# Two batches by halves: a sliding-window attention with a feed-forward layer, its first loads, casts and transposes cut in two

## The chip, the cores and the metric

The kernel runs on one core of a Trainium2 chip. The metric is the device time of one execution in microseconds (us). The core has a matrix engine (TensorE, PE in the profile, with PEld for its weight loads), VectorE (DVE), ScalarE (ACT), GpSimd (POOL) and SyncE (SP), which here only issues DMAs. Each engine works through its own queue in order; semaphores tie the queues together.

## The reference

```python
# q, k, v: [8 batches, 8 heads, 576 tokens, 64], float32
scores = q @ k.T / 8                                   # per batch and head
scores = where(|i - j| <= 32, scores, -1e9)            # a band of 65 keys a query
attn   = softmax(scores) @ v
x      = attn transposed and reshaped to [4608, 512]   # 8 heads side by side
h      = x @ w_in                                      # [4608, 2048]
out    = maximum(0.01 * h, h) @ w_out                  # [4608, 512], float32
```

## The kernel before, in words

Heads go in pairs: two heads of 64 fill 128 partitions, so a batch has four pairs (`NPAIR`). The work is a chain of **steps**, one pair and one stretch of tokens each. Steps 0 to 15 (`OLD`) belong to batches 0 and 1: a batch has two halves of 288 tokens (`HALF`), and steps 0 to 3 are half 0 of batch 0, pair by pair, 4 to 7 its half 1, 8 to 15 batch 1. Steps from 16 on take four blocks of 64 tokens of batches 2 to 7 in another form (`score_blocks`, `product_blocks`), with queries and keys transposed by DMA. The parts of an early step:

- `score`: TensorE multiplies blocks of 64 keys with the queries that can see them into the one score tile `ps`, ScalarE takes the exponential into `e`, GpSimd multiplies with a mask (line 442) into one of six `prob` tiles.
- `sums`: TensorE sums over keys with a block matrix of ones (line 466), VectorE takes the reciprocal (line 471).
- `product`: TensorE multiplies with values (line 482) into the one tile `x`; `scaled`: VectorE multiplies with the reciprocal (line 496) into `xT`, the input of the feed-forward layer.

For batches 0 and 1, `load_qk` (line 80) brings a pair's queries and keys as float32 with 96 partitions of six tokens, `cast_qk` (lines 279 and 281) makes bfloat16 of them in `qb` and `kb`, and `transposes` turns them on TensorE (line 327), with ScalarE taking them out of the accumulators (lines 335 and 341). Queries and keys of a pair are separate tiles, and the queries of batches 0 and 1 are kept apart by even and odd tokens. Values come by `load_v` (line 104) in two DMAs of 64 partitions a pair, and `cast_v` puts them into a block-diagonal tile `vbd` that was cleared before. Batch 1 has block-diagonal keys `kbd` too (`place_keys`, line 359). SP issues all these loads in program order; the weights go by GpSimd's queue (`load_w_in`, line 675, and `load_w_out`, line 679), each in four pieces, cast on the way.

The feed-forward layer takes **groups** of tokens: groups 0 to 3 are the four halves of batches 0 and 1. For each of 16 tiles `f` of 128 hidden features, TensorE adds four chunks (one per pair, line 520), and ScalarE applies the leaky ReLU (`h_out`, line 531) into `gT`. `h_first` opens four tiles at once and goes chunk by chunk, so that a chunk can begin when its pair is done. Output tiles of 128 tokens take 16 matmuls with `w_out` (lines 593 and 609).

The order is written out by hand up to the end of group 1: casts, transposes, `score`, `sums`, `product` and `scaled` of batch 0, with dummy matmuls (`keep_busy`, line 622) in between; then the tiles of group 0 with steps 4 to 7 (`second_half`) among them; then group 1 with transposes of batch 1 (`second_pair`) and the score of step 8. From there a plan interleaves the tiles with the steps: `spend` is called before each tile or quarter of an output tile (a **turn**), runs the steps that are due (step 8 in the seventh turn, 9 in the ninth, then 10 and 11), and in the first turns some extra work of batch 1. `step` also casts and transposes queries and keys of batch 2 and later by `qk_due` and issues later loads by `qk_next`, `v_next`. Batch 2's transposed queries are copied into `qz` by `place_queries` (line 315); `qz`, `kz` and `vw` of batches 2 and up share memory (two `sets`) with the tiles of batches 0 and 1, and the zeros in `qz` are written by `clear_half` (lines 234 and 239).

The opening of the order before, which sets when the loads are asked for:

```python
load_qk(0, 0); load_qk(0, 1); load_v(0, 0)
load_qk(0, 2); load_qk(0, 3)
for p in range(1, NPAIR):
    load_v(0, p)
```

Of the kernel before, what the change touches and what calls it, by code (L numbers as in the profile page):

```python
# [16 lines left out]
def kernel(  # L17
# [14 lines left out]

    nc = tc.nc
# [12 lines left out]
    EVEN = HALF // 2  # L46
# [22 lines left out]
    def load_qk(b, p, behind=None):  # L69

        for into, src, name in ((qf, q, "qf"), (kf, k, "kf")):
            t = fload.tile([96, 2, RUN * D], FP32, name=f"{name}{p}")
            if behind is not None:
                behind.memset(t[0:1, 0, 0:1], 0.0)
                behind = None
            heads = src[b, 2 * p:2 * p + 2]
            if b < BY_DMA:
                nc.sync.dma_start(out=t, in_=heads.rearrange("a (p c) d -> p a (c d)", c=RUN))  # L80
            elif into is qf:
# [9 lines left out]
            into[b, p] = t  # L91
# [9 lines left out]
    def load_v(b, p):  # L101
        t = vf[b, p]
        for a in range(2):
            nc.sync.dma_start(
                out=t[64 * a:64 * a + 64],
                in_=v[b, 2 * p + a].rearrange("(c p) d -> p c d", p=64),
# [28 lines left out]
    qb = const.tile([96, NPAIR, RUN, 2, D], BF16)  # L135
    kb = const.tile([96, NPAIR, RUN, 2, D], BF16)
# [5 lines left out]
    qT, kbd, vbd, qz, kz, vw, vw_two = [], [], [], [], [], [], []  # L142
    for t, at in zip(sets, (0, NPAIR * S)):
        qT.append(sets[0][:, at:at + NPAIR * S].rearrange("p (n s) -> p n s", n=NPAIR))
# [22 lines left out]
    def clear(t, p):  # L167
# [4 lines left out]

    mask = [const.tile([128, 2, 2, EVEN], BF16, name=f"mask{i}") for i in range(2)]
    nc.vector.memset(mask[0][:, 1, :, 0:16], 0.0)
    nc.vector.memset(mask[1][:, 1, :, 128:EVEN], 0.0)
# [7 lines left out]
        [((0, 0, 48), (2, 48, 64), (4, 112, 32)), ((1, 16, 64), (3, 80, 64))],  # L183
        [((4, 0, 32), (6, 32, 64), (8, 96, 48)), ((5, 0, 64), (7, 64, 64))],
    ]

    win = sets[1][:, N_SET - 384:].rearrange("p (c m i) -> p c m i", c=2, m=3)
    nc.gpsimd.memset(win, 1.0)
    for lo in (0, 64):
# [3 lines left out]
            base=0, channel_multiplier=-1, pattern=[[1, 2], [0, 3], [2, 64]],  # L193
# [3 lines left out]
            base=2 * W, channel_multiplier=1, pattern=[[-1, 2], [0, 3], [-2, 64]],  # L197
        )
    nc.gpsimd.memset(vbd[0][:, 3], 0.0)
    win_f = win.rearrange("p c m i -> p c (m i)")  # L200

    def make_mask(hf):
        lo = (16, 32)[hf]
        nc.gpsimd.tensor_copy(out=mask[hf][:, 0], in_=win_f[:, :, lo:lo + EVEN])
        lo = (16, 0)[hf]
        nc.gpsimd.tensor_copy(out=mask[hf][:, 1, :, lo:lo + 128], in_=win_f[:, :, 0:128])
# [49 lines left out]
    prob = const.tile([128, NPROB, 2, 2, EVEN], BF16)  # L256
# [3 lines left out]
    ps_v = ps[:, P0:P0 + 2 * HALF].rearrange("p (n c i) -> p n c i", n=2, c=2)  # L260
# [14 lines left out]
    def cast_qk(b, p, q_eng=None):  # L275
        for eng, src, dst in ((q_eng or nc.gpsimd, qf, qb), (nc.gpsimd, kf, kb)):
            to, tok = dst[:, p], src[b, p].rearrange("p a (c d) -> p c a d", d=D)
            if eng is nc.scalar:
                eng.activation(out=to, in_=tok, func=AF.Copy)
            else:  # L280
                eng.tensor_copy(out=to, in_=tok)  # L281

    def cast_v(b, p, on_act=False, heads=range(2), eng=nc.gpsimd):
        for a in heads:
            r = slice(64 * a, 64 * a + 64)
            if on_act:
                nc.scalar.activation(out=vbd[b % 2][r, p, :, r], in_=vf[b, p][r], func=AF.Copy)  # L287
            else:
                eng.tensor_copy(out=vbd[b % 2][r, p, :, r], in_=vf[b, p][r])
# [8 lines left out]
    def transpose_dma(b, p):  # L298
        t = kt.tile([128, S], BF16, name="kT")
        for to, src in ((t, qb), (kz[b % 2][:, p, W:W + S], kb)):  # L300
            nc.sync.dma_start_transpose(
                out=to.rearrange("p (c i) -> p c i", c=RUN),
                in_=src[:, p].rearrange("p c a d -> p (c a d)"),
            )
        landing.append((base(b) - 4 + p, b, p, t))
# [12 lines left out]
    def transposes(b):  # L318

        for p in range(NPAIR):  # L320
            for which, src in (("q", qb), ("k", kb)):
                if (b, p) == (1, 2):
                    tp = xps.tile([128, RUN, 96], BF16, name="tp", tag="sx"[which == "q"])
                else:
                    tp = mmps.tile([128, RUN, 96], BF16, name="tp", tag="mm")
                for c in range(RUN):
                    nc.tensor.transpose(
                        tp[:, c],
                        src[:, p, c].rearrange("p a d -> p (a d)"),
                        ident[0:96, 0:96],  # L330
                    )

                tok = tp.rearrange("p (e c) i -> p c i e", c=2)
                if which == "q":
                    nc.scalar.activation(
# [568 lines left out]
```

## Time and profile before

| | before |
|---|---|
| median of three runs | 314.26 us (313.77 to 315.05) |
| the profiled execution | 314.13 us |
| its span in the profile | 312.3 us |
| TensorE busy | 298.2 us (95%) |
| VectorE busy | 221.6 us (71%) |
| ScalarE busy | 212.6 us (68%) |
| GpSimd busy | 199.1 us (64%) |
| DMA | 49.47 MB, mean 158 GB/s |
| matmuls of the hidden layer, line 520 | 133.2 us |
| output matmuls, line 593 | 122.5 us |

The span runs from the first to the last instruction that the profile holds; the time of an execution has 1.83 us more around it. Shares are of the span. A row of the timeline reads: start, length, engine, line and operation, output and input, and in brackets how long the engine had stood idle before it and what released it. A row of the windows reads: stretch, length, then busy time with number of instructions for PE, PEld, DVE, ACT and POOL, the granted clock of TensorE, the DMA share and GB/s. The queue q1 of the DMA view carries what SP issues, q0 what GpSimd issues.

### The profile page before, as it was taken

To read this page: it belongs to the slowest core of one execution; us is meant where nothing else is said; L and a number is where in the kernel's file an instruction comes from. 1 tells how busy PE (TensorE), PEld (TensorE's weight loads), DVE (VectorE), ACT (ScalarE), POOL (GpSimd) and SP (SyncE) were. 2 spreads that over 40 slices of the span, in tenths; PEclk is the share of its full clock that TensorE was granted. 3 is DMA by queue.
4 is the path that set the end of the run, shared out by engine and by line. 5 is a ranking of instruction groups with operands and counts; after the bars stand their busy time and mean duration, and the time that the engine had idled before them with its cause. 6 is when DMAs were issued, how large, how long until landed. Compare 5 with 4: busy or idle time off the path is not lost.

```text
span 312.3 us, 6748 instructions
## 1 busy us (share of the span) xinstructions
PE 298.2 (95%) x2516; PEld 194.8 (62%) x2545; DVE 221.6 (71%) x290; ACT 212.6 (68%) x434; POOL 199.1 (64%) x250
## 2 busy tenths in 40 slices
PE   1799999999999999999999999999999999999996
PEld 1577775585765858585959585858555555544643
DVE  3688959779768887898789767898679866743000
ACT  7687698583865858585949686858589548842731
POOL 7789936899799999488778357578947622110000
PEclk9999999999999999999999999999999999999999
DMA  8999999998999799989989995797950011001002
GB/s 181 224 217 227 268 249 198 204 216 143 211 216 216 145 266 174 206 174 251 198 145 186 257 230 101 163 209 144 206 129 0 33 67 41 0 36 68 34 28 75
DMA packets 122017, 49.47 MB, mean 158 GB/s; under 512 B 96256, under 2 KB 117504, under 8 KB 121984
## 3 DMA queue, kind: packets, MB, share of 16 engines
q1 hardware_dynamic: 117760, 44.84, 72.7%
q0 software_dynamic: 4224, 4.19, 8.0%
q8 instruction: 20, 0.33, 0.5%
q14 instruction: 13, 0.11, 0.1%
HBM read 36.70 MB, written 9.44 MB: 148 GB/s over the span
## 4 chain that ended last, share of the span: by engine, by line
PE 77%; POOL 10%; DMA 5%; ACT 3%; SPq 2%; issue 2%; DVE 1%; POOLq 0%; ACTq 0%; DVEq 0%
PE mm L520 34%; PE mm L593 31%; PE ps L380 3%; DMA kf<-in_k_dram 2%; PE mm L609 2%; POOL prob L387 2%; PE s L398 2%; POOL kb L281 2%; PE x L398 2%; POOL qb L281 2%; DMA set<-kb 1%; ACT set L287 1%; POOL prob L442 1%; DMA vbuf<-in_v_dram 1%; SPq L80 1%
## 5 line engine op out<-in xcount | busy, mean ns | idle before, releaser
L520 PE MATMUL mm<-xT,w_in_bf 128*128 128x256 bf16 (+3 forms) x956 | 133.2, 294 | 0.4
L593 PE MATMUL mm<-w_out_bf,gT 128*128 128x512 bf16 (+2 forms) x537 | 122.5, 373 | 1.3
L407 DVE RECIPROCAL r<-r 128x256 f32<-128x256 f32 (+1 forms) x56 | 94.9, 1696 | 37.3 <-ACT r L406 36.9
L520 PEld LDWEIGHTS <-w_in_bf 128*128 128x128 bf16 x960 | 91.4, 98 | 30.6 <-issue 0.6
L387 POOL TENSOR_TENSOR prob<-e,band 128x512 bf16<-128x512 bf16 (+1 forms) x56 | 62.6, 1117 | 56.0 <-ACT e L385 54.6
L593 PEld LDWEIGHTS <-gT 128*128 128x128 bf16 x560 | 52.0, 98 | 54.1
L531 ACT ACTIVATE gT<-mm 128x288 bf16<-128x288 f32 (+2 forms) x112 | 49.8, 479 | 12.3 <-PE mm L520 9.6
L385 ACT ACTIVATE e<-ps 128x512 bf16<-128x512 f32 (+1 forms) x56 | 32.4, 579 | 27.7 <-PE ps L380 27.0
L598 ACT ACTIVATE o_sb<-mm 128x512 f32<-128x512 f32 (+2 forms) x35 | 20.5, 585 | 38.5 <-PE mm L593 38.2
L554 ACT ACTIVATE gT<-mm 128x512 bf16<-128x512 f32 x64 | 35.7, 596 | 5.5 <-PE mm L520 4.2
L471 DVE RECIPROCAL r<-s 128x288 f32<-128x288 f32 x16 | 31.2, 1950 | 2.9 <-PE s L466 2.8
L281 POOL CAST kb<-kf 96x768 bf16<-96x768 f32 x32 | 27.2, 851 | 9.2 <-DMA kf<-in_k_dram 8.1
L411 DVE TENSOR_TENSOR xT<-x,r 64x256 bf16<-64x256 f32 (+1 forms) x56 | 24.3, 435 | 3.3
L411 DVE TENSOR_TENSOR xT<-s,r 64x256 bf16<-64x256 f32 (+1 forms) x56 | 24.3, 434 | 3.3
L442 POOL TENSOR_TENSOR prob<-e,mask 128x576 bf16<-128x576 bf16 x16 | 20.3, 1273 | 5.9 <-ACT e L440 4.9
L315 DVE COPY set<-kT 64x576 bf16<-64x576 bf16 x48 | 21.4, 446 | 2.1 <-DMA kT<-qb 1.2
L380 PEld LDWEIGHTS <-set 128*128 128x128 bf16 x216 | 16.7, 98 | 9.6 <-DMA set<-kb 0.4
L380 PE MATMUL ps<-set 128*128 128x128 bf16 x216 | 21.4, 219 | 0.2 <-DMA set<-kb 0.2
L281 POOL CAST qb<-qf 96x768 bf16<-96x768 f32 x24 | 19.6, 819 | 0.8 <-DMA qf<-in_q_dram 0.8
L294 POOL CAST set<-vbuf 128x640 bf16<-128x640 f32 x24 | 17.2, 716 | 3.1 <-DVE r L407 1.7
L398 PEld LDWEIGHTS <-set 128*128 128x128 bf16 x432 | 18.0, 98 | 0.5
L295 POOL CAST set<-vbuf 64x512 bf16<-64x512 f32 x24 | 14.8, 615 | 1.5
(84 smaller groups left out, 237.0 us busy)
## 6 DMA issues: line engine op xcount, KB each, us to landing
qf<-in_q_dram SPq DMA_DIRECT2D x32, 288.0 KB, 5.9
kf<-in_k_dram SPq DMA_DIRECT2D x32, 288.0 KB, 6.6
out_dram<-o_sb SPq DMA_DIRECT2D x35, 256.0 KB, 2.7
vbuf<-in_v_dram SPq DMA_DIRECT2D x15, 256.0 KB, 4.7
vbuf<-in_v_dram SPq DMA_DIRECT2D x16, 144.0 KB, 7.0
w_in_bf<-in_moe_w_in_dram POOLq DMA_DIRECT2D x4, 512.0 KB, 8.2
w_out_bf<-in_moe_w_out_dram POOLq DMA_DIRECT2D x4, 512.0 KB, 15.5
vbuf<-in_v_dram SPq DMA_DIRECT2D x10, 192.0 KB, 4.5
```

The lines of the kernel that those rows point to most:

```text
L281: eng.tensor_copy(out=to, in_=tok)
L380: nc.tensor.matmul(sc[:, :, w], kz[b % 2][:, p, 64 * m:64 * m + 128], tok[:, :, :, at:at + 32], start=True, stop=True,)
L385: nc.scalar.activation(out=e[:, 0:n], in_=ps[:, lo:lo + n], func=AF.Exp, scale=scale)
L387: nc.gpsimd.tensor_mul(pr, e[:, 0:n], band.rearrange("p w c i -> p (w c i)")[:, 0:n])
L398: nc.tensor.matmul(x[:, a, w], vw[b % 2][:, p, m, a:a + 2].rearrange("p n d -> p (n d)"), pr[:, a, w], start=True, stop=True,)
L407: nc.vector.reciprocal(r[:, 0:n], r[:, 0:n])
L411: nc.vector.tensor_mul(xT[rows, p, t0:t0 + n].rearrange("p (w i c) -> p w c i", i=32, c=2), x[rows, a].rearrange("p (w c i) -> p w c i", c ...
L471: nc.vector.reciprocal(r, s)
L520: nc.tensor.matmul(h[:, 0:n], w_in_bf[:, c, ts(f, 128)], xT[:, c, t0:t0 + n], start=(c == 0), stop=(c == DMC - 1),)
L531: nc.scalar.activation(out=to, in_=h, func=AF.Prelu, alpha=0.01)
L554: nc.scalar.activation(out=gT[:, f - 1:f + 1, t0:t0 + 256], in_=hh.rearrange("p (f t) -> p f t", f=2), func=AF.Prelu, alpha=0.01,)
L593: nc.tensor.matmul(o[:, lo:hi], gT[:, f, t0:t0 + 128], w_out_bf[:, f, lo:hi], start=(f == 0), stop=(f == FFC - 1),)
```

## The change

Batches 0 and 1 are loaded, cast and transposed by halves of tokens instead of by queries and keys. A half of a pair has the queries of its 288 tokens in 48 partitions and the keys that they need in 64 (half 0, 384 keys) or 32 more (half 1, the other 192); both lie in one tile, are cast by one instruction and leave the accumulator in one piece of 672 or 480 columns. Values are loaded and cast in two parts, blocks 0 to 4 and 5 to 8. In batch 0 all first halves come first. In batch 1 the first halves come pair by pair, the second halves two pairs in one load, the first two pairs' ahead of the values.

```diff
-    def load_qk(b, p, behind=None):
+    def load_half(b, p, hf, pairs=1, behind=None):
+        r = slice(2 * p, 2 * (p + pairs))
+        t = loaded[hf][:, r]
...
+        k0, kn = 384 * hf, KROWS[hf]
+        for src, row, t0, n in ((q, 0, HALF * hf, QROWS), (k, QROWS, k0, kn)):
+            nc.sync.dma_start(
+                out=t[row:row + n],
+                in_=src[b, r, t0:t0 + RUN * n].rearrange("a (p c) d -> p a (c d)", c=RUN),
+            )
...
-    load_qk(0, 0)
-    load_qk(0, 1)
-    load_v(0, 0)
-    load_qk(0, 2)
-    load_qk(0, 3)
+    load_half(0, 0, 0)
+    load_half(0, 1, 0)
+    load_v(0, 0, 0, 5)
+    load_half(0, 2, 0)
+    load_half(0, 3, 0)
     for p in range(1, NPAIR):
-        load_v(0, p)
+        load_v(0, p, 0, 5)
+    for p in range(NPAIR):
+        load_half(0, p, 1)
+    for p in range(NPAIR):
+        load_v(0, p, 5, NB)
```

Tokens stay in their natural order, so the masks, the products and `h_out` lose their split by parity (`h_out` writes straight into `gT`). The mask is a call of its own, `mask_out`, and step 0's runs on VectorE. The opening begins with dummies that need only the matrix of ones, and is written anew (cut to its first half; the rest goes on in the same way up to `score(5)`, with second halves' casts on ScalarE and transposes among the steps):

```diff
+    def warm_up(n, pool=xps, tag="x"):
+        t = pool.tile([128, 512], FP32, name=tag, tag=tag)
         for _ in range(n):
             nc.tensor.matmul(
+                t[:, 0:128], ones_bd, ones_bd, start=True, stop=True, skip_group_check=True,
+            )
...
+    warm_up(24)
+    clear_half(0, 0, 0, nc.vector)
+    clear_half(0, 0, 1, nc.vector)
+    cast_half(0, 0, 0, nc.vector)
     make_mask(0)
+    make_mask(1)
+    cast_half(0, 1, 0, nc.vector)
+    transposes(0, 0, 0)
+    warm_up(5)
+    score(0, nc.vector)
+    transposes(0, 1, 0)
+    warm_up(8)
+    cast_v(0, 0, nc.vector, hi=5)
+    cast_half(0, 2, 0, nc.gpsimd)
+    load_w_in(0, 512)
+    mask_out(0)
+    score(1)
     sums(0)
+    transposes(0, 2, 0)
     product(0)
+    keep_busy(ps, 0, 5)
     scaled(0)
+    mask_out(1)
+    cast_half(0, 3, 0, nc.scalar)
+    cast_v(0, 1, nc.scalar, nc.gpsimd, hi=5)
+    score(2)
+    warm_up(5, mmps, "mm")
     sums(1)
+    transposes(0, 3, 0)
+    mask_out(2)
     load_w_in(512, 1024)
+    product(1)
+    keep_busy(ps, 0, 5)
+    scaled(1)
+    cast_v(0, 2, nc.scalar, nc.gpsimd, hi=5)
+    cast_half(0, 0, 1, nc.scalar)
+    score(3)
+    h0 = h_first(0, 2)
+    h = next(h0)
+    keep_busy(h, HALF, 3)
+    sums(2)
+    transposes(0, 0, 1)
+    mask_out(3)
     load_w_in(1024, 1536)
+    product(2)
+    keep_busy(h, HALF, 12)
+    scaled(2)
+    next(h0)
...
```

`h_first(0, 2)` opens two tiles of group 0 instead of four. The other 14 tiles go in stretches of 2, 3, 4 and 5, each followed by a step:

```diff
+    f = 2
+    for i, n in zip(range(NPAIR, 2 * NPAIR), (2, 3, 4, 5)):
+        for f in range(f, f + n):
+            h_tile(0, f)
+        f += 1
+        if i < 6:
+            score(i + 2)
+        product(i)
+        scaled(i)
+        if i < 7:
+            sums(i + 1)
+        if i == 4:
+            transposes(0, 3, 1)
+        if i < 6:
+            mask_out(i + 2)
+        if i < 7:
+            cast_v(0, i - 3, nc.scalar, nc.gpsimd, lo=5)
+            load_w_out(i - 4)
+        if i == 4:
+            for n in range(NPAIR):
+                load_half(1, n, 0, 1, nc.gpsimd if n == 0 else None)
...
+    load_w_out(3)
+    load_half(1, 0, 1, 2)
+    for p in range(NPAIR):
+        load_v(1, p, 0, 5)
+    load_half(1, 2, 1, 2)
+    load_v(1, 0, 5, NB)
+    for p in range(NPAIR):
+        nc.gpsimd.memset(kbd[1][:, p], 0.0)
+    clear_half(0, 2, 0, nc.vector)
+    clear_half(0, 2, 1, nc.vector)
+    cast_half(1, 0, 0, nc.vector)
+    cast_half(1, 1, 0, nc.vector)
...
```

In group 1 the first halves of batch 1 are transposed after tiles 5, 8, 11 and 14 (`transpose_part`), and casts of pairs 2 and 3 follow on VectorE (`cast_part`). The second halves are cast on GpSimd in turns 3, 5, 7 and 8 (`CASTS`), with the rest of the values and batch 2's queries and keys loaded behind each cast, and transposed in turns 6, 8, 11 and 13 (`PARTS`). The fills: the zeros of `qz[0]` are written by VectorE in the opening and after step 7 (before by ScalarE and GpSimd in the second and fourth turn and in step 14), those of `qz[1]` by VectorE in steps 16 to 19 (before in the opening); the band for steps 16 and up is made by GpSimd in group 1 (before in steps 10 to 12). Batch 2's copies of queries come one step later:

```diff
-        landing.append((base(b) - 4 + p, b, p, t))
+        landing.append((base(b) - (3 if b == BY_DMA else 4) + p, b, p, t))
...
+        if OLD - 2 < i <= OLD:
+            place_queries()
         weighted(i)
-        place_keys()
         place_queries()
...
-        if i == OLD - 2:
-            for a in range(2):
-                clear_half(0, 2, a, nc.gpsimd)
+        if OLD <= i < OLD + NPAIR:
+            clear_half(1, (i - OLD) // 2 * 2, i % 2, nc.vector)
```

More of the change, by code (lines that the diff above doesn't have):

```diff
@@ L67, with load_qk @@
     BY_DMA = 2
-    def load_qk(b, p, behind=None):
+    loaded = [fload.tile([112, H, RUN * D], FP32, name=name) for name in ("qf", "kf")]
+    def load_qk(b, p, pairs=1):
+        r = slice(2 * p, 2 * (p + pairs))
         for into, src, name in ((qf, q, "qf"), (kf, k, "kf")):
[L74 to L81, printed above, removed]
+            t = loaded[into is kf][0:96, r]
+            heads = src[b, r]
+            if into is qf:
                 nc.sync.dma_start(
@@ L90, in load_qk @@
                 )
-            into[b, p] = t
+            for i in range(pairs):
+                into[b, p + i] = t[:, 2 * i:2 * i + 2]
+    QROWS, KROWS = 48, (64, 32)
+    halves = {}
+    def load_half(b, p, hf, pairs=1, behind=None):
+        r = slice(2 * p, 2 * (p + pairs))
+        t = loaded[hf][:, r]
+        if behind is not None:
+            behind.memset(t[0:1, 0, 0:1], 0.0)
+        k0, kn = 384 * hf, KROWS[hf]
[4 more added lines that the diff above has]
+            )
+        for i in range(pairs):
+            halves[b, p + i, hf] = t[0:QROWS + kn, 2 * i:2 * i + 2]
     vbuf = const.tile([128, NPAIR, 10 * D], FP32)
@@ new lines, in keys, with place_keys @@
+    def keys(b, p, blk):
+        at = HALF + 64 * blk if blk < 6 else halves_at(1) + HALF + 64 * (blk - 6)
+        return qk[b][:, p, at:at + 64]
+    landing = []
+    def place_keys(p, hf):
+        n, at = KROWS[hf] * RUN, halves_at(hf) + HALF
+        for a in range(2):
+            r = slice(64 * a, 64 * a + 64)
+            nc.vector.tensor_copy(
+                out=kbd[1][r, p, 6 * hf:6 * hf + n // 64, r],
+                in_=qk[1][r, p, at:at + n].rearrange("p (n j) -> p n j", j=64))
```

328 lines of the change are left out of this document (130 added, 198 removed).

## The prediction

> **What bounds the kernel now.** I read the busy table and the slices of the page first, then the windows, then the timeline of the first 60 us, and last the DMA view by five-microsecond windows.
>
> ```profile
> PE 298.2 (95%) x2516; PEld 194.8 (62%) x2545; DVE 221.6 (71%) x290; ACT 212.6 (68%) x434; POOL 199.1 (64%) x250
> PE   1799999999999999999999999999999999999996
> 24.00:36.00 12.00, 11.86 (x121) 8.88 (x119) 10.57 (x11) 7.47 (x20) 11.90 (x14) 1.00 1.19 244
> 116.00:312.30 196.30, 192.25 (x1547) 121.96 (x1566) 132.57 (x173) 129.40 (x267) 102.58 (x123) 1.00 0.64 127
> ```
>
> TensorE (first column of the windows after the length) is full from about 25 us to the end. Only the first slices are thin. So the time is the moment at which TensorE becomes full, plus the work then left, plus later holes. The timeline of the opening shows what holds it back:
>
> ```profile
> 5.73 0.66 PE L327 MATMUL tp<-ident,qb 96*128 96x96 bf16 x6 [5.73 <-DVE qb L281]
> 11.88 1.96 DVE L471 RECIPROCAL r<-s 128x288 f32<-128x288 f32 x1 [1.23 <-PE s L466]
> 12.43 0.81 POOL L281 CAST kb<-kf 96x768 bf16<-96x768 f32 x1 [0.42 <-DMA kf<-in_k_dram]
> 14.97 0.82 POOL L281 CAST kb<-kf 96x768 bf16<-96x768 f32 x1 [0.49 <-DMA kf<-in_k_dram]
> 15.21 1.96 DVE L471 RECIPROCAL r<-s 128x288 f32<-128x288 f32 x1 [0.82 <-PE s L466]
> 18.94 1.96 DVE L471 RECIPROCAL r<-s 128x288 f32<-128x288 f32 x1 [0.36 <-PE s L466]
> 22.39 1.95 DVE L471 RECIPROCAL r<-s 128x288 f32<-128x288 f32 x1
> 24.96 0.65 PE L520 MATMUL mm<-xT,w_in_bf 128*128 128x288 bf16 x4
> 34.09 2.08 PE L520 MATMUL mm<-xT,w_in_bf 128*128 128x288 bf16 x15
> ```
>
> The reciprocals of steps 0 to 3 start at 11.88, 15.21, 18.94 and 22.39 (step 4 at 24.86). After step 3 comes the last chunk of group 0's first tiles (24.96), and from there TensorE runs without a hole into group 1 (34.09). Keys of pairs 2 and 3 are waited for until 12.4 and 15.0. One reciprocal and its scaling cost VectorE 1.96 + 0.46 = 2.42 us, and the steps follow every 3.2: queues and landings set the pace, not VectorE alone.
>
> DMA by windows, 20 to 25 us, 30 to 35 us and 50 to 55 us:
>
> ```profile
> q1 hardware_dynamic: 16, 0.00, 0.6%
> q1 hardware_dynamic: 548, 0.77, 50.4%
> q1 hardware_dynamic: 3075, 1.06, 112.1%
> ```
>
> SP's loads are all in by 20 us. While the weights move on the other queue they get 0.155 MB/us (0.77 in 5 us), later 0.21.
>
> **Landings in the opening.** Before, pair 0's queries land at 4.14 (issue 0.82, 3.3 us to landing). After that 2.36 MB land by 14.95 (keys of pair 3), so 0.22 MB/us; I use 0.21. A pair's first half is (48+64) rows x 2 heads x 1,536 B = 0.344 MB instead of 0.590, a first part of values 0.164. Counting on at 0.21: pair 0 at 4.4, pair 1 at 6.0, values 0 at 6.8, pair 2 at 8.4, pair 3 at 10.1 (before 5.2, 8.45, 9.8, 12.4, 15.0), the first second half at about 14. SP has twice the issues: 16 more at 0.45 (queries and keys) and 0.65 (values) are 8.8 us of SP. The first ten stand where they stood; the rest makes the first second half 14.4 instead of 13.6, and the last values 22.5, wanted at 23.
> The Trainium skill (DMA: Bandwidth & Descriptors, Rules for kernel authors) speaks against this: two transfers to disjoint partition halves gain nothing, and small ones should be joined. The trace bears it out in part: the two value loads of 0.147 MB landed 0.87 us apart (9.04, 9.91), 0.17 MB/us against 0.21; loads of 0.066 to 0.082 MB it does not show.
>
> **Walk through the opening.** Durations from the timeline: cast 0.56 (1.53 while POOL works beside it), eviction of a transposed half 0.73 (0.65 at 576 columns), exp 0.65, mask on POOL 1.27, six transposes 0.66 early and 0.42 later (about 0.27 start to start). The mask of step 0 on VectorE is not in the trace; the nearest row is the joined add, 0.31 to 0.90 for 288 columns, so 0.6 to 1.8; I take 0.65.
> Cast of pair 0 4.4 to 5.9, transposes to 6.5, evicted 7.35, score and exp to 8.55, mask to 9.3, the second score first in TensorE's order, sums 9.8, reciprocal 0 at 10.25. Step 1: mask on POOL 10.55 to 11.8, then sums behind the third score: 12.9. Step 2: exp 12.75 (ScalarE has a cast and half a value cast ahead of it), mask to 14.75: 15.5. Step 3: exp waits on ScalarE for the first cast of a second half, 14.6 to 15.4; mask to 17.4; TensorE has twelve dummies and the first chunk of group 0 (first weights issued 9.3, 8.2 us to landing, 17.5) and a score ahead: 19.15. Step 4: 21.6, and the last chunk of step 3 starts at 21.6 too. Before it was 24.96: 3.4 us.
> TensorE warm early is part of this: six transposes, ten score matmuls and two sums cost 0.66 each until 16.7 us and 0.42 after 18.5, when dummies had run. The early dummies lie in time in which TensorE waits (5.73 us before its first transpose). If they do not work: +1.0 (four groups at 0.24 on the chain). The twelve dummies cost 0.9 at worst; none is in the later path.
>
> **What is then left for TensorE.** Before, from 24.96 to 34.09: 52 matmuls at 0.122 (16 in 1.97 from 27.83), 2 scores at 0.36, 4 products and 3 sums at 0.24: 8.74, and 0.39 of small holes. After: two tiles less are open in the first chunks, so 58 matmuls, the same steps, and two more half transposes at 0.27: 10.0, with the holes 10.4. Group 1 begins at 32.0 instead of 34.09: **2.1 us gained**. VectorE's last scaling, 21.6 + 4 x 2.42 and small waits, ends at 32 as well, needed 1.5 us later. The last input weights, issued 20.7, land 28.5 to 30.4 and are wanted at 29.5: 0 to 0.9 us.
>
> **Group 1 and batch 1.** Transposes: four half sets in group 1 and four in the turns, before as many of 96 columns: 0. Output of group 0 to 3 written straight instead of by parity: ScalarE 0.41 each, off the path; 0.
> Loads: POOL's trigger moves from 25.07 to about 27, behind a mask, a value cast and the first output weights. At 0.155 MB/us from 29.6 the first halves land at 31.8, 34.0, 36.2, 38.4; TensorE wants them cast by 34.5, 36.2, 38.0, 39.8. The VectorE casts stand behind two fills (2 x 0.54) and last 0.6 to 1.5 beside POOL's six fills of 1.06. A TensorE wait of 0 to 1.5 is the bound; I take 0.1. Values and second halves: pairs 0 and 1 at 41.6, values 42.6 to 45.8, pairs 2 and 3 at 48.5; POOL asks for these in the third to eighth turn (43 to 48.5) and TensorE from 46 to 54. POOL is blocked for a microsecond, behind it masks 10 and 11, needed two steps on. 0 taken, up to 1.
> Batch 2's queries and keys are issued after 43; they reach SP at 49.10 now, because SP stands behind value loads. Not later; 0, and up to 0.6 gained: the two holes at 54.4 and 55.6 are that large together.
>
> **Fills.** Four clears of 0.54 move on VectorE from the opening to steps 16 to 19, where it has 7.92 us of work in 12 (80 to 92 us). Clears leave ScalarE (1.16) and POOL (1.05, 2.17); the band's three pieces (0.52, 0.73, 0.73) move on POOL from 61 to 70 us into group 1, where POOL works 3.50 of 9.35. Hidden at both ends; without the cover up to 1. Batch 2's query copies (0.90) come one step later, in the step before their score. VectorE then has 0.9 + 0.3 + 1.95 + 0.46 = 3.6 per step, and the steps come every 4.0 (66.94, 70.97, 74.95 on TensorE): it fits by 0.4. If not, the score of step 16 waits, up to 0.9.
>
> **Sum.** 314.13 for the profiled execution (span 312.3, 1.83 around it): -2.1 opening, +0.1 casts, -0.2 of the two holes: 311.9. The median of the three runs is 314.26, 0.13 above; a measurement of this kernel can tell about 0.5%, 1.57 us, so faster means below 312.7.
>
> **Rivals.**
> *The steps follow faster.* If ScalarE and POOL keep VectorE's pace of 2.42 from 10.25, step 4 starts at 19.95, 1.6 earlier: 310.2. For it: POOL and ScalarE are only some 80% full in my walk. Against: the first weights at 17.5. 0.14.
> *The opening gives little.* The dummies do not lift the pace (1.0) and the last weights come late (0.9): 2.2 falls to 0.3, 313.8. 0.12.
> *Halves land no sooner than wholes.* With twice the loads at the rate of the value loads and worse, pairs 2 and 3 come at 12.4 and 15.0 as now, steps 3 and 4 stay where they are, and the six matmuls and two transposes more for TensorE are not paid for: 314.13 + 1.3 - 0.2 = 315.2. Against: 0.17 is only a fifth under 0.21, and pair 3's first half has 1.54 MB ahead of it and in it, where the whole has 2.65. 0.06. This is where the rule of the Trainium skill on joined transfers (DMA: Bandwidth & Descriptors, Rules for kernel authors) would lead; the loads here are of both kinds that it warns of.
> *Batch 1 starves, slower.* One mechanism: the hardware queue's share beside the output weights, which are now issued from 26 to 31 instead of 23.5 to 28.5. At 0.12 MB/us the first half of pair 3 lands at 41.1 and TensorE waits 1.9; the rest, 1.63 MB, lands at 54.7 where 52 is the latest, 2.6 more: 4.5 lost against 2.2, 316.4. It decides below 0.135 MB/us. For it: the pairs of batch 1 are waited for by POOL now (2.8 and 2.9 us at 41.5 and 45.3), and lead from trigger to first use shrinks from 10.4 to 6 us. Against: 0.15 held for 15 us, and only 58% is needed at first. 0.18.
>
> **The numbers.** Forecast as worked out 0.50, of which 0.04 lie above 312.7. Faster 0.46 + 0.14 = 0.60; same 0.04 + 0.18 = 0.22; slower 0.18. The range leaves out the worst of starving and the very best: 308.9 to 315.6.
>
> **What would show it.** Right: reciprocals near 10.3, 13, 15.5, 19, 21.6; first group-1 matmul near 32; no TensorE wait over 0.5 us on a cast or landing from 32 to 56. Wrong: step 3's reciprocal after 21, transposes of batch 1 waiting on VectorE or POOL casts, or a hole at scores 16 to 19 behind the query copies.

## The result: slower by 2.7%, where a gain of 0.7% was forecast

| | before | after |
|---|---|---|
| median | 314.65 us (4 runs, 313.77 to 315.17) | 322.64 us (4 runs, 321.64 to 323.24) |
| ratio | 1 | 1.0268 [1.0245, 1.0292] |
| profiled execution, its span | 314.13, 312.3 us | 322.52, 320.8 us |
| first matmul of group 1 | 34.09 | 37.85 (+3.8) |
| first output tile | 44.09 | 52.00 (+7.9) |
| score of step 16 | 71.09 | 79.75 (+8.7) |

The forecast was 311.9 (308.9 to 315.6). The page of the profile after: the busy row, then TensorE's row and its clock in 40 slices.

```profile
PE 305.7 (95%) x2591; PEld 200.0 (62%) x2591; DVE 226.9 (71%) x303; ACT 212.9 (66%) x444; POOL 196.1 (61%) x251
...
PE   6958969999999999999999999999999999999996
...
PEclk9979979999999999999999999999999999999999
```

The loss is in the first seven slices of 8 us: the third and the sixth are thin in TensorE's row, and the clock is at 7 in the same two. The last 196.3 us are those of before (192.25 us of TensorE then, 193.18 now). The windows give the places (columns as before: TensorE, its loads, VectorE, ScalarE, POOL, then clock, DMA share and GB/s):

```profile
15.00:20.00 5.00, 1.21 (x17) 0.59 (x18) 3.16 (x3) 1.17 (x3) 1.48 (x3) 0.99 1.17 229
20.00:25.00 5.00, 5.00 (x52) 3.93 (x52) 1.14 (x2) 2.95 (x6) 2.64 (x4) 0.67 1.11 190
30.00:35.00 5.00, 4.89 (x56) 3.69 (x54) 4.28 (x3) 4.45 (x12) 4.39 (x7) 1.00 0.63 101
40.00:45.00 5.00, 1.91 (x15) 1.37 (x15) 5.00 (x2) 1.68 (x6) 4.86 (x7) 0.88 1.16 265
45.00:50.00 5.00, 5.00 (x41) 3.74 (x40) 3.25 (x9) 3.84 (x9) 0.77 (x1) 0.78 1.21 218
124.50:320.80 196.30, 193.18 (x1568) 121.99 (x1565) 132.48 (x173) 129.25 (x267) 104.07 (x125) 1.00 0.59 128
```

Three things stand out: TensorE idle in 15 to 20 us, DMA down to 101 GB/s in 30 to 35 (before 267), and TensorE idle again in 40 to 45. After each hole the clock is lower for some microseconds (0.67 in 20 to 25 us, 0.78 in 45 to 50). The timeline shows what ended the first and the second hole:

```profile
10.67 1.96 DVE L485 RECIPROCAL r<-s 128x288 f32<-128x288 f32 x1 [1.48 <-PE s L480]
13.84 1.96 DVE L485 RECIPROCAL r<-s 128x288 f32<-128x288 f32 x1 [0.65 <-PE s L480]
16.31 1.96 DVE L485 RECIPROCAL r<-s 128x288 f32<-128x288 f32 x1
19.05 0.84 ACT L295 ACTIVATE kb<-kf 80x768 bf16<-80x768 f32 x1 [3.83 <-DMA kf<-in_k_dram]
20.78 2.44 PE L640 MATMUL mm<-mask,ones_bd 128*128 128x224 bf16 x12
24.32 1.96 DVE L485 RECIPROCAL r<-s 128x288 f32<-128x288 f32 x1 [2.84 <-PE s L480]
32.39 0.09 POOL L97 MEMSET qf<- 1x1 f32 x1
37.25 4.05 POOL L797 MEMSET set<- 128x1152 bf16 x4
37.85 3.40 PE L533 MATMUL mm<-xT,w_in_bf 128*128 128x288 bf16 x24
39.85 5.33 DVE L297 CAST qb<-qf 112x768 bf16<-112x768 f32 x2
41.24 2.06 POOL L803 MEMSET set<- 128x1152 bf16 x2
44.23 0.74 PE L348 MATMUL tp<-ident,qb 112*128 112x112 bf16 x6 [2.98 <-DVE qb L297]
44.77 2.83 PE L533 MATMUL mm<-xT,w_in_bf 128*128 128x288 bf16 x12
```

- **First hole.** Steps 0 to 2 come early, as forecast. Then ScalarE stands 3.83 us at the cast of pair 0's second half, which has not landed, and the exponential of step 3 is behind it. The first chunk's twelve dummies, at the clock of 0.67, take 2.44 us (1.31 in the run f4 below, where the clock was 1.00). Step 3's reciprocal is 5 us behind the forecast.
- **Second hole.** Two VectorE casts that take 0.56 us each by themselves take 5.33 us together, over POOL's fills, and TensorE waits 2.98 us for the first. Twelve matmuls then take 2.83 us (1.64 for the next twelve). These two, 2.98 + 1.19, are what group 1 lost: it takes 14.15 us to the first output tile, before 10.00.

The third place is not in TensorE's row. POOL's trigger for batch 1 (32.39, before 25.07) is behind the late steps. SP waits for it, no longer than before (9.8 us then), but until 32.51 instead of 25.19:

```profile
SPq L100 <- POOL qf L97: 8.0, 1, 8.0
```

SP's rows of the timeline show what follows. Before (values of batch 1, then batch 2's first queries):

```profile
31.41 17.59 SPq L104 DMA_DIRECT2D vbuf<-in_v_dram  x8
49.10 0.58 SPq L82 DMA_DIRECT2D qf<-in_q_dram  x1
```

After (first parts of values, second halves, second parts, batch 2's first queries):

```profile
39.14 12.57 SPq L118 DMA_DIRECT2D vbuf<-in_v_dram  x8
51.80 0.84 SPq L100 DMA_DIRECT2D kf<-in_q_dram  x1
53.33 0.32 SPq L100 DMA_DIRECT2D kf<-in_k_dram  x1
53.74 2.61 SPq L118 DMA_DIRECT2D vbuf<-in_v_dram  x4
56.45 0.55 SPq L77 DMA_DIRECT2D qf<-in_q_dram  x1
```

Batch 2's loads are issued 7.35 us later than before, and the trigger alone is 7.32 later: from there to batch 2's first load SP took 23.9 us in both kernels. The queue q1 in 20 to 25 and in 50 to 55 us:

```profile
q1 hardware_dynamic: 1536, 0.46, 41.8%
q1 hardware_dynamic: 2521, 0.88, 85.9%
```

Before it had 0.00, then 0.77 in 30 to 35 us, then 1.06. Now loads of batch 0 are still moving at 25 us, and in 30 to 35 there is no row of q1 at all.

### The profile page after: what moved, and what is told of

Its sections match the earlier page's. It is cut to its first block, busy times and chain, and to the rows that moved or that the text cites. A ratio compares the mean times of both kernels' runs of the same rounds, so it can differ in the third digit from the quotient of the medians.

```text
span 320.8 us, 6954 instructions
## 1 busy us (share of the span) xinstructions
PE 305.7 (95%) x2591; PEld 200.0 (62%) x2591; DVE 226.9 (71%) x303; ACT 212.9 (66%) x444; POOL 196.1 (61%) x251
## 4 chain that ended last, share of the span: by engine, by line
PE 83%; DVE 4%; SPq 3%; DMA 2%; POOL 2%; issue 2%; ACT 2%; POOLq 0%; ACTq 0%; DVEq 0%
PE mm L604 36%; PE mm L533 34%; PE ps L389 4%; DMA kf<-in_k_dram 2%; PE mm L620 2%; PE x L407 2%; PE s L407 2%; SPq L100 2%; SPq L118 2%; DVE qb L297 1%; POOL prob L455 1%; DVE r L485 1%; PE tp L348 1%; PE x L495 1%; PE mm L640 1%
## 5 line engine op out<-in xcount | busy, mean ns | idle before, releaser
L533 PE MATMUL mm<-xT,w_in_bf 128*128 128x256 bf16 (+3 forms) x960 | 135.5, 296 | 0.7 <-DVE xT L509 0.4
L604 PE MATMUL mm<-w_out_bf,gT 128*128 128x512 bf16 (+2 forms) x560 | 124.6, 373 | 0.0
L455 POOL TENSOR_TENSOR prob<-e,mask 128x576 bf16<-128x576 bf16 x15 | 19.1, 1272 | 18.5 <-ACT e L449 16.5
L297 POOL CAST kb<-kf 96x768 bf16<-96x768 f32 (+1 forms) x29 | 23.9, 826 | 1.2 <-DMA kf<-in_k_dram 1.2
L297 POOL CAST qb<-qf 96x768 bf16<-96x768 f32 (+1 forms) x25 | 20.6, 822 | 4.5 <-DMA qf<-in_q_dram 2.7
L337 DVE COPY set<-kT 64x576 bf16<-64x576 bf16 x48 | 21.4, 447 | 1.8 <-DMA kT<-qb 0.8
L352 ACT ACTIVATE set<-tp 128x672 bf16<-128x672 bf16 (+1 forms) x16 | 10.4, 650 | 8.2 <-PE tp L348 7.9
```

Of the source, the lines that this page charges most:

```text
L297: eng.tensor_copy(out=to, in_=src)
L533: nc.tensor.matmul(h[:, 0:n], w_in_bf[:, c, ts(f, 128)], xT[:, c, t0:t0 + n], start=(c == 0), stop=(c == DMC - 1),)
L604: nc.tensor.matmul(o[:, lo:hi], gT[:, f, t0:t0 + 128], w_out_bf[:, f, lo:hi], start=(f == 0), stop=(f == FFC - 1),)
```

## The experiments

Theories. **A**: the late landing of the second halves, with ScalarE's queue behind it, costs the opening. **B**: POOL's fills lock VectorE's casts out. **C**: the loads of batch 2, chained behind a late opening and behind batch 1's extra pieces, set the end whatever TensorE gains earlier. Offsets below are to the profile of before: group 1's first matmul 34.09, first output tile 44.09, batch 2's first load 49.10, score of step 16 71.09. Versions with the same code up to there showed step 3's reciprocal anywhere from 20.38 to 23.62, so an offset of one profile is good to some 2 us, and the ratios decide. On time alone e1 to e4, f2 and g4 cannot be told from the kernel after (1.0245 to 1.0292); what they show is where a wait went.

### Casts moved, fills moved

`e1_late_cast` moves the casts of second halves behind step 3:

```diff
-    cast_half(0, 0, 1, nc.scalar)
     score(3)
...
+    cast_half(0, 0, 1, nc.scalar)
+    cast_half(0, 1, 1, nc.scalar)
+    transposes(0, 0, 1)
+    score(4)
```

> Only the opening's order is changed: ScalarE casts the first second half (pair 0 of batch 0) after the exponential of step 3 instead of before it, and its transposes, the score of step 4 and what hangs on them follow the sums of step 3. Theory A (ScalarE's queue stood 3.83 us on the landing of that half at 18.9, with the exponential of step 3 behind it, and TensorE's clock fell in the hole): the exponential of step 3 near 15.5 instead of 19.8, reciprocal of step 4 near 23 instead of 26.8, first matmul of group 1 near 34 instead of 37.9, time 318 to 319. Rival (VectorE's and GpSimd's pace sets the opening, and the wait only stands in front of it): under 1 us gained, 321.5 to 322.5.

Measured 322.60 us, ratio 1.0261 [1.0234, 1.0289]. Step 3's reciprocal came at 18.39 instead of 24.32, step 4's at 24.69, and group 1 began only 1.1 us earlier: steps 4 and up need the late halves too. So the order of ScalarE's queue was not the cause. The landing is left, and f4 below moves it.

`e2_act_casts` gives the two casts that were locked out to ScalarE:

```diff
-    cast_half(1, 0, 0, nc.vector)
-    cast_half(1, 1, 0, nc.vector)
+    cast_half(1, 0, 0, nc.scalar)
+    cast_half(1, 1, 0, nc.scalar)
```

> Only the first two casts of batch 1 move, from VectorE to ScalarE. Theory B (VectorE's cast of 112x768 cannot run while GpSimd's fills of the block-diagonal tiles run back to back, and took 4.4 us instead of 0.56): ScalarE does each in 0.85, the 2.98 us wait of the first transposes of batch 1 is gone, and TensorE's clock stays up there; time 319 to 319.5. Rival (the halves of batch 1 had landed late, or ScalarE is late itself): the wait stays with another name, 321.5 to 322.6.

Measured 321.77, 1.0247 [1.0220, 1.0274]. The 2.98 us hole is gone and the first output tile stands at +4.3 instead of +7.9, but step 16 is at +6.4 and the end at +7.0. A shorter wait took the place of the hole: TensorE stands 1.51 us at 41.07 for the leaky ReLU, which is behind the two casts on ScalarE.

`e3_both` has both edits.

> Late cast in the opening and the two casts of batch 1 on ScalarE together. Theories A and B: the gains add, 7 to 8 us, 314.5 to 316. If the one wait only covers for the other, the gain is that of the larger one, 318.5 to 319.

Measured 321.45, 1.0234 [1.0195, 1.0274]. The first output tile comes 4.3 us earlier than in the kernel after (+3.6), and step 16 takes most of it back. Its score in TensorE's timeline:

```profile
77.56 0.58 PE L389 MATMUL ps<-set 128*128 128x128 bf16 x4 [2.55 <-DVE set L337]
```

L337 copies the transposed queries of batch 2; its first load was issued at 55.42. By the next steps the loss was +8.1. That is theory C.

`e4_dve_fills` leaves the casts on VectorE and moves the six fills of `kbd` and `vbd` that POOL had to VectorE, behind the casts (two more of `vbd` were there already).

> The casts of batch 1 stay on VectorE, but the eight fills of its block-diagonal tiles stand behind them on VectorE too, so that GpSimd has none of them. Theory B (the shared access, not the place in VectorE's queue or the landing): both casts take 0.56 to 0.9, the first transposes of batch 1 follow tile 5 without a wait over 0.5; the score of step 8 may wait for the key fill by under 1 us; time 319 to 320. Rival (late landing): the cast still ends near 44, 322 to 323.

Measured 321.75, 1.0244 [1.0211, 1.0276]. The same two casts in the timeline:

```profile
39.42 0.95 DVE L297 CAST qb<-qf 112x768 bf16<-112x768 f32 x2
```

0.95 us instead of 5.33, on the same engine in the same place, with no fills beside them: B is shown. The time stayed above the 319 to 320 that was expected: the next cast now stood behind the fills on VectorE, TensorE waited 1.90 us for it at 46.26, and the first output tile came only 1.3 us earlier (50.72). The Trainium skill (SBUF — State Buffer, Who interferes with whom) has the rule: VectorE's fast casts and POOL share a pair of ports, whoever has it keeps it for a whole instruction and the other blocks. The trace agrees, and goes further: the cast did not get in between two fills, but waited through the rest of four, two more and another of 0.52 us (43.24 to 43.76), and was done at 44.18. VectorE's clears at 38.69 and 39.38 kept their 0.54 us beside the same fills.

### Earlier loads and another order of loads

`f2_early_loads` moves batch 1's trigger from step 4 to just behind the last piece of `load_w_in`; `f1_both_early_loads` is that with the edits of e3.

```diff
     load_w_in(1536, 2048)
+    for n in range(NPAIR):
+        load_half(1, n, 0, 1, nc.gpsimd if n == 0 else None)
```

> Late cast and the two casts on ScalarE as before, and the loads of batch 1's first halves are triggered on GpSimd behind the fourth piece of input weights (about 22 to 24 us) instead of behind step 4's work at 31. Theory C (from 24 to 75 us the loads set the time: SP stood 6 to 8 us on that trigger, the DMA engines moved 0.5 MB between 30 and 35 us where before it was 1.34, so batch 2's queries are asked for at 55.4 instead of 49.1 whatever TensorE does earlier, and the score of step 16 waits): batch 2's first load at 48 to 50, the score of step 16 at 72 to 74 instead of 77.6, time 315 to 317. Rival (batch 2's loads are late because the two-part values and halves cost more in SP's queue, not for the trigger): first load of batch 2 still after 53, 320 to 321.5.

> Only the trigger of batch 1's first halves is moved forward, nothing else. Theory C with the blocked cast of VectorE kept: the opening and the 3 us hole before batch 1's transposes stay, the supply is earlier by 6 to 8 us; the two are in series, so TensorE's hole now bounds: 320 to 321.5. Rival (theory C alone sets the time): 317 or less.

Measured: f2 322.38, 1.0246 [1.0210, 1.0282]; f1 319.57, 1.0171 [1.0131, 1.0211]. Alone, the trigger gains nothing (TensorE is as late, the first output tile at 51.64); with TensorE earlier it gains 1.9 us on e3's 321.45 (in another comparison; the intervals of the ratios overlap), and the loss at step 16 falls from +6.5 to +3.4. Two bounds stood one behind the other, and neither shows before the other is lifted. f1 also parts the late start from the added loads: SP starts on batch 1 at 25.02, as before (25.19), and still asks for batch 2 only at 54.13, 5.0 us later.

`f4_load_order` changes only the order of batch 0's loads:

```diff
-    for p in range(1, NPAIR):
-        load_v(0, p, 0, 5)
-    for p in range(NPAIR):
-        load_half(0, p, 1)
+    load_v(0, 1, 0, 5)
+    load_half(0, 0, 1, 2)
+    load_v(0, 2, 0, 5)
+    load_v(0, 3, 0, 5)
+    load_half(0, 2, 1, 2)
```

> Only the order of batch 0's loads on SP is changed: the second halves' queries and keys of pairs 0 and 1 in one load each behind the values of pair 1, those of pairs 2 and 3 behind the values of pair 3. Theory A' (the first second half landed at 18.9 because eight issues of values and small loads stood ahead of it on SP until 11.3, and the first weights then shared the engines): it lands near 14, ScalarE waits under 1 us, reciprocal of step 3 near 19 and of step 4 near 22, group 1 starts near 34; with the trigger of batch 1's loads some 3 us earlier too, time 318.5 to 320. Rival (the weights of 9.9 us take the engines whatever the order): landing after 17, 321.5 or more.

Measured 320.18, 1.0181 [1.0139, 1.0223]. ScalarE's cast of the first second half, in the timeline, starts 3.8 us earlier and without a wait:

```profile
15.28 0.83 ACT L296 ACTIVATE kb<-kf 80x768 bf16<-80x768 f32 x1
```

Step 3's reciprocal came at 21.17, step 4's at 23.97, and group 1 at 36.05 (after 37.85). The half landed at 13.62 instead of 18.97, with the first weights asked for at the same time (9.83 and 9.89), so the rival, that the weights take the engines whatever the order, is out. What waits now is a value cast (3.07 us at 20.33). So A holds, with the landing as its cause: 1.8 us at group 1 in this profile, 2.5 us in the medians, and the intervals of the ratios do not touch. The loads joined in pairs are what the Trainium skill (DMA: Bandwidth & Descriptors, Rules for kernel authors) asks for; place and size were changed together here, so the run does not show which of the two helped.

`f5_all` is f4's order, f2's trigger and e2's casts.

> The load order of batch 0, the trigger forward and the two casts on ScalarE together, the opening's order otherwise as in the changed kernel. If theories A', B and C are the whole loss: TensorE reaches group 1 near 33, batch 2's first load before 50, time 312 to 315. If something else holds it (query copies one step late, the dummies, ScalarE's longer queue): 316 to 319, with the wait of the score of step 16 still there.

Measured 318.22, 1.0121 [1.0090, 1.0153]. The first output tile is at +1.3, step 16 at +1.7, step 22 at +3.7, the span at +4.0. Over half of the loss is mended. TensorE still waits 0.99 us at 33.48 for the last input weights, and a part of what is left comes after the first output tile. POOL's timeline has that part, at the cast of batch 2's first values:

```profile
76.29 0.72 POOL L317 CAST set<-vbuf 128x640 bf16<-128x640 f32 x1 [4.88 <-DMA vbuf<-in_v_dram]
```

`g1_best_try` adds e1's order, an earlier last piece of `load_w_in`, and batch 2's loads ahead of the second parts of values; `g2_all_swap` adds only the last to f5.

> Everything learned so far put together on the changed kernel: load order of batch 0, late cast, the trigger of batch 1's loads forward, its first two casts on ScalarE, the last input weights asked for right behind the third piece, and batch 2's queries and keys asked for ahead of the rest of batch 1's values. If the supply up to step 16 is all that is left of the loss (4.1 us in the run with all three repairs): 314.5 to 316.5, with the score of step 16 within 1 us of the kernel before. If ScalarE's queue is now the limit: 317 to 319.

> The run with load order, trigger and ScalarE casts, and in it only batch 2's queries and keys ahead of the rest of batch 1's values on SP. Theory C (SP's order sets when batch 2 comes): each of batch 2's loads 1 to 2 us earlier, the 2.4 us lost between steps 16 and 22 shrink to about 1, time 316.5 to 317.5. Rival (the DMA engines are full there, so order is no gain, or the late values now hold steps 12 to 15): 318 to 319.5.

Measured: g1 319.77, 1.0142 [1.0095, 1.0190]; g2 317.95, 1.0099 [1.0068, 1.0130]. Neither beats f5 beyond its interval. In g1 a late value load held the opening: ScalarE waited 3.62 us for it at 19.26 and TensorE 3.81 for the cast of another at 19.45. Step 3's reciprocal came at 23.33, and step 4's, behind it in e1's order, at 28.37.

### What holds batch 2

`h1_values_other_queue` issues batch 1's values on ScalarE's queue, `h2_no_twelve` drops the twelve dummies ahead of the first chunk, `h3_queue_no_twelve` does both, `h4_whole_values` has h2's edit and batch 1's values in whole pieces (8 loads for 16). All start from f5.

```diff
-            nc.sync.dma_start(
+            (nc.sync if b == 0 else nc.scalar).dma_start(
                 out=t[64 * a:64 * a + 64, lo:hi],
```

> The version with all three repairs (load order of batch 0, early trigger, casts of batch 1's first two halves on ScalarE; 318.22 before), with batch 1's values issued on ScalarE's DMA queue instead of SP's. If SP's order holds batch 2: its first load comes before 50 us instead of 52.9, the values of batch 2 no later than in the kernel before by more than 2 us, the loss at steps 16 to 22 shrinks from 3.7 to about 1.5, 316. If the DMA engines are full: batch 2's data land as late as before, 318.

> The version with all three repairs, without the twelve dummies ahead of the first chunk of group 0. If they stand on TensorE's path: group 1 begins about 1 us sooner than 35.7 and the time falls by 0.5 to 1 us (317.2 to 317.7); if step 16's supply decides, 318.2 as before.

> Both: values of batch 1 on the other queue, no twelve dummies. SP's order and TensorE both decide: 315 to 315.5. If the engines are full: 318.

> The version with all three repairs, without the twelve dummies, and with batch 1's values in whole pieces on SP's queue (8 loads of 0.147 MB instead of 16). If the number of issues in SP's line decides: batch 2's first load about 3 us sooner (8 issues of 0.4 us fewer), near 50, and 316 to 316.5. If the engines are full or the place in the queue decides: 317.5 to 318, since the second halves of pairs 2 and 3 now come behind more bytes.

Measured: h1 332.87, 1.0573 [1.0536, 1.0610]; h2 319.42, 1.0154 [1.0113, 1.0195]; h3 331.91, 1.0549 [1.0505, 1.0593]; h4 319.04, 1.0133 [1.0084, 1.0183]. The dummies are no cost that the time shows (h2 is not faster than f5). h1 failed in an instructive way; ScalarE's timeline, its DMA queue first:

```profile
36.92 14.56 ACTq L118 DMA_DIRECT2D vbuf<-in_v_dram  x10
51.53 1.57 ACT L296 ACTIVATE qb<-qf 112x768 bf16<-112x768 f32 x2 [14.21 <-DMA vbuf<-in_v_dram]
```

Ten value loads kept their issuer for 14.56 us. On SP, in f5, the eight first parts took 12 us; on ScalarE the leaky ReLU stood behind them, and TensorE stood still for 14.38 us. The issues are not slow in themselves: each of the ten takes 0.60 to 0.69 us. The rest is waiting for earlier transfers: the sixth, seventh and tenth start within 0.02 us of the landing of the first, second and fourth (44.63, 46.59, 50.86), whose semaphores they use again. The Trainium skill (DMA: Bandwidth & Descriptors, Issuing engines are not separate DMA queues) says that issuing from another engine only saves issue time, usually small beside the DMA. The trace agrees that nothing comes sooner (the eighth first part landed at 52.91, in f5 at 52.29), but here the wait to issue was that of the transfers and stopped an engine that computes. h4, with eight issues fewer and the same bytes, asked for batch 2 at 52.06 instead of f5's 52.87: so it is not the number of issues.

`i1_no_second_values` and `i2_no_values` take the bytes away.

> The version with all three repairs (318.22), without the loads of the second parts of batch 1's values (the products of batch 1's last four blocks use batch 0's values). If bytes ahead of batch 2's loads decide: batch 2's first load near 50 instead of 52.9, its values about 3 us sooner than 71.05, the loss at step 22 falls from 3.7 to 1.5 or 2, 316 to 316.5. If it is something else in steps 16 to 22: 318.

> The same without any load of batch 1's values (its products use batch 0's). SP then has nothing between batch 1's queries and keys and batch 2's. If bytes ahead of batch 2 decide: batch 2's first load follows the cast of its tile, 48 to 49, and the end stands at the offset of the first output tile, +1.0 to 1.5: 315.5 to 316. If it is something else: 318.

Measured: i1 316.93, 1.0075 [1.0039, 1.0111]; i2 318.56, 1.0127 [1.0078, 1.0175]. In i1 batch 2's first load was asked for at 48.31 (52.87 in f5), 23.0 us after SP began on batch 1 (23.9 in the kernel before). It landed no sooner (57.41, in f5 57.15), but the last keys of batch 2 landed 1.7 us earlier and its first values were asked for 1.6 earlier; their cast, at 75.24, waited for no DMA. The first output tile was at +2.9 in this profile, step 16 at +3.7, and the end at +3.3. TensorE's waits from 60 to 100 us, in f5:

```profile
PE x L408 <- DVE xT L510: 0.8, 1, 0.8
PE s L408 <- POOL prob L397: 0.5, 1, 0.5
PE ps L390 <- DVE set L338: 0.4, 1, 0.4
PE x L408 <- POOL prob L397: 0.3, 1, 0.3
```

and in i1:

```profile
PE mm L534 <- DVE xT L510: 0.4, 1, 0.4
```

f5 lost 2.0 us from step 16 to step 22, i1 and i2 nothing. i1 reached step 16 2.0 us later than f5, which alone leaves the loads more time; but f1, with all of batch 1's values, reached it about as late (+3.4) and lost 2.0 on the way to step 22. So in these profiles the bytes of batch 1 ahead of batch 2 are the last term; the time does not show it, for the intervals of the ratios of i1 and f5 overlap. i2 missed: with all of batch 1's values gone its profile shows a wait of 1.37 us for output weights at 50.23, and the time rose by 1.6 us over i1. Why those weights came later with fewer bytes beside them is open.

### The dummies

`g4_no_dummies` is the kernel after without any dummy matmuls in the opening; `g3_before_dummies` is the kernel before with one line more, `warm_up(24)` ahead of the first cast.

> The changed kernel without any of the dummy matmuls of the opening (42 of 128 columns, 25 of 224). If they shorten the chain by the warm clock: TensorE cold up to group 0's tiles and beyond, 1 to 2.5 us slower, 323.5 to 325. If the 3.8 us hole behind the late half cools the clock anyway and the rest only fills waits: within 0.7 us of the changed kernel, or up to 1 us faster for the twelve that ran cold in 2.4 us.

> The kernel before with one part of the change alone: 24 early dummies on TensorE that need only the matrix of ones. If a warm clock from 6 us on is worth something by itself: transposes and scores of steps 0 to 2 at 0.42 instead of 0.66, 0.3 to 1.0 us gained, 313.0 to 313.8. If loads and the chain of exponentials set the pace there: within 0.3 us of the kernel before.

Measured: g4 321.58, 1.0206 [1.0161, 1.0251], group 1 at 35.0 instead of 37.85, but the end at +8.3. In the late opening the dummies took TensorE time (a part of the 2.85 us is that the first second half landed at 17.67 here, 18.97 in the kernel after); behind the first output tile the gain is lost again, as in e3. g3 313.69, 0.9974 [0.9954, 0.9994], 10 runs against 15: **the best version**, 0.8 us under its kernel before (314.47). TensorE's timeline of g3:

```profile
2.24 2.74 PE L621 MATMUL x<-ones_bd 128*128 128x128 bf16 x24 [2.24 <-DVE ones_bd L161]
4.77 0.67 PE L327 MATMUL tp<-ident,qb 96*128 96x96 bf16 x6
6.50 0.43 PE L327 MATMUL tp<-ident,kb 96*128 96x96 bf16 x6 [1.06 <-POOL kb L281]
12.00 0.69 PE L327 MATMUL tp<-ident,qb 96*128 96x96 bf16 x6
33.30 4.46 PE L520 MATMUL mm<-xT,w_in_bf 128*128 128x288 bf16 x32
43.29 1.03 PE L609 MATMUL mm<-w_out_bf,gT 128*128 128x512 bf16 x4
```

The four groups from 6.50 to 8.50 take 0.43 to 0.51 us where they took 0.66; then TensorE stands 1.39 us, and from 10.41 to 15.5 the groups take 0.64 to 0.69 again. Group 1 and the first output tile come 0.8 us earlier in this profile. But its loads, which the edit does not touch, also landed earlier (pair 1's queries at 6.41, before 7.08; pair 3's keys at 13.34, before 14.92), and its first transposes start at 4.77 instead of 5.73. So the gain is measured (half of what the prediction took as the least that can be told, but the interval, of 25 runs, leaves 1 out); that the clock is its cause is not shown.

## Why the prediction was wrong

- **Landings in the opening: the failed step.** "The first second half at about 14", made 14.4, landed near 19. The first halves were right: the first three reciprocals came at 10.67, 13.84 and 16.31 for 10.25, 12.9 and 15.5. The rate of 0.21 MB/us was carried on past the point where the first weights start on the other queue, and over six value loads in pieces of 256 bytes. The DMA view of 10 to 15 us, after:

```profile
q0 software_dynamic: 506, 0.51, 68.5%
q1 hardware_dynamic: 1197, 0.29, 26.2%
```

  The loads got 0.06 MB/us there; the second halves were issued from 11.27 and landed over 7 us later, and the last values at 28.8 instead of 22.5. The 0.155 that the prediction used beside weights for batch 1 would not have saved it: 0.74 MB after pair 3's first half at that rate is a landing at 15. With two of the six value loads ahead instead (f4) the loads moved 0.63 MB in the same 5 us, beside 0.34 of weights.
- **Walk through the opening, "exp waits on ScalarE for the first cast of a second half, 14.6 to 15.4".** The dependence was seen, and priced with the wrong landing: 3.83 us of standing instead of none, on an in-order queue. But e1 shows that the queue was not the point.
- **"What is left", group 1 at 32.0.** It came at 37.85. The earliest of all versions by halves was 34.64 (h3), still behind before's 34.09; why is open. The term of -2.1 was wrong in sign.
- **Group 1: "a TensorE wait of 0 to 1.5 is the bound; I take 0.1".** It was 2.98 of waiting and 1.19 of clock. The bound came from a cast of 1.53 that met a single POOL fill. The profile of before has the longer case: six fills back to back, and a cast that began with the last of them and was done 0.4 us behind it.

```profile
30.49 6.04 POOL L774 MEMSET set<- 128x1152 bf16 x6
35.52 2.53 DVE L281 CAST qb<-qf 96x768 bf16<-96x768 f32 x2
```

  The first of these casts took 1.44 us (35.52 to 36.95), because only 1.0 us of the run was left. The upper end should have been the run of fills, and the band's first piece, which the term on fills called hidden in group 1, is its end (43.24 to 43.76).
- **The trigger "to about 27"** followed from the opening's dates and came at 32.39. DMA stood partly idle in 30 to 35 us.
- **"Batch 2's queries and keys ... Not later; 0".** 7.35 later. The text knew that SP stood behind value loads; it did not add the shift of the chain's start, which in the kernel after is the whole of it (7.32), nor batch 1's second halves and second parts, which the change puts ahead of batch 2 (51.80 to 56.35 in SP's rows) and which cost 5.0 us once the start is as early as before (f1). Late supply makes the repairs of the first two terms give little: e3 had 4.3 us at the first output tile and kept 1.2 in the median.
- **Near:** the early dummies, put at 1.0, gave 0.8 on the kernel before (g3), but the clock is not shown as the cause. The twelve dummies, "0.9 at worst", took 2.44 in the late opening of the kernel after, but cost nothing that can be measured in f5 (h2). The fills and query copies at steps 16 to 19 took nothing: step 16 was at +8.7 and the next three at +8.6 to +8.7.
- **The rivals.** "Batch 1 starves" had the sign and the kind (loads behind a late start), with the wrong place and price: it is batch 2 that starves, by the order of SP's queue and the bytes ahead, and it put 316.4. No rival held the lock.

Worked out on the profiles: +3.76 to group 1, +4.15 in group 1 (lock and clock), +0.75 to step 16, and -0.1 behind it, 8.5 together. By the versions (differences of medians), the lock and the landing are on the path only as far as supply lets them be: f4 alone regains 2.5 us, e2 alone 0.9 and f2 alone 0.3 (neither can be told from nothing), all three together (f5) 4.4, and with 0.52 MB fewer (i1) 5.7. What holds the rest is open.

## What to carry to other kernels

When a load is cut in two so that one half comes sooner, price the second half with the rate that is left beside everything else then in flight, and follow its bytes down the same queue to the next batch's loads. Where two bounds follow each other, undoing one shows nothing: undo both, then each. Keep a fast VectorE cast that something waits for out of a run of POOL instructions, or give it to ScalarE, whose own queue then pays for it (1.51 us in e2).

## What the runs showed of the hardware

- Two VectorE casts (0.56 us each alone) took 4.2 us more beside a run of POOL fills (5.33; 0.95 without the fills, e4); the first was done 0.4 us after the run had ended, in the kernel after and in the kernel before.
- Issuing loads can hold an engine far longer than the issues take: 14.56 us on ScalarE for ten value loads of at most 0.082 MB, of which each issue is 0.60 to 0.69; three times the issue waited for an earlier load of the same semaphore to land (h1). On SP single issues of value loads took up to 2.32 us (f5, at 41.13) where 0.6 is usual.
- After holes of 3.68 and 2.98 us in the kernel after TensorE's granted clock was 0.67 (20 to 25 us) and 0.78 (45 to 50). After a hole of 2.99 us in f4 (up to 42.43) it was 1.00, and the same six transposes took 0.47 instead of 0.74. What tells the two apart is open.
- In g3 24 dummies (2.24 to 4.98) were followed by groups at 0.43 to 0.51 up to 9.0 us, and from 10.41 at 0.64 to 0.69 again, at a granted clock of 0.50 in 10 to 15 us. The profile of before gives a clock of 1.00 in 5 to 15 us although its matmuls take 0.66 there, so the lengths are the surer sign.
